# Moving the w3 weight load from the SyncE DMA queue to the ScalarE DMA queue in a one-core decode kernel

## The chip, the cores and the metric

The kernel runs on one core of one Trainium2 chip. The metric is the device time of one execution in microseconds (us), as the median of several executions; a profile of one execution, with every instruction and every DMA packet, goes with each kernel. When two kernels are compared by a ratio, it is the mean time of the one kernel's runs over that of the other's in the same rounds, so it is not quite the ratio of the medians that are quoted beside it.

## The reference, cut to what matters

One token (sequence length 1) goes through two branches that are added: attention over a key/value cache of 65,536 positions in 4 groups, and an MLP.

```python
x  = A_x                                    # 1 x 1 x 1024
xn = _layernorm(x)
return x + _A_ref(xn, k_cache, v_cache, wq, wo) + _B_ref(xn, w1, w2, w3, w4)

# A: q = xn @ wq; softmax(q k / sqrt(128)) v for 32 heads over 4 cache groups; @ wo
# B:
h  = _gelu(_layernorm(x) @ w1)
g0 = jnp.pad(h[:, :, 0*c:1*c], ((0, 0), (1, 0), (0, 0)))[:, :S, :]   # and three more shifts
hs = jnp.concatenate([g0, g1, g2, g3], axis=-1) @ w2
x1 = x + hs
h2 = _gelu(_layernorm(x1) @ w3) @ w4
return x1 + h2
```

All tensors are bfloat16. The bytes: wq 8.4 MB, w3 7.3 MB, w1 and w2 2.1 MB each, 8 key and 8 value blocks of 8.4 MB each, wo 8.4 MB, w4 7.3 MB. That is 169.87 MB for one token, each byte used once.

## The kernel before

Everything that comes from memory passes through three large buffers ("slots", `SLOTS = 3`) in one fixed order. When a matrix or a block has been used up, `done` frees its slot and the next load of the stream is issued into it. All the large loads are issued by the SyncE queue; only the 2 KB row x comes through the ScalarE queue.

```python
    stream = ["wq", "w3", "w12"]
    for u in range(NU):                      # NU = 8 blocks
        ...                                  # cut: the last block has wo between K and V
            stream += [("K", u), ("V", u)]
    stream.append("w4")

    class Stream:
        def pump(self):
            while self.next < len(stream) and self.held < SLOTS:
                ...                          # cut: take the next one
                self.load(it)
        def done(self, it):
            self.tiles.pop(it)
            self.held -= 1
            self.pump()
        def load(self, it):
            t = big.tile([P, ROW], BF16, name="big")
            self.tiles[it] = t
            go = nc.sync.dma_start
            if it == "wq":
                go(out=t[:], in_=A_wq.rearrange("(p c) n -> p (c n)", c=DC))
            elif it == "w3":
                go(out=t[:, 0:DC * F], in_=B_w3.rearrange("(p c) f -> p (c f)", c=DC))
            elif it == "w12":
                go(out=t[:, 0:DC * D], in_=B_w1.rearrange("(p c) n -> p (c n)", c=DC))
                go(out=t[:, DC * D:2 * DC * D], in_=B_w2.rearrange("(m c) n -> m (c n)", c=DC))
            ...                              # cut: wo, w4
            else:
                kind, i = it
                g, b = divmod(i, NB)
                cache = A_k_cache if kind == "K" else A_v_cache
                go(out=t[:], in_=cache[0, g, b * UKEYS:(b + 1) * UKEYS, :].rearrange("(p ct) d -> p (ct d)", p=P))
    ...
    nc.scalar.dma_start(out=x_row[0:1, :], in_=A_x[0, 0:1, :])
    st.pump()
```

So the first key block waits for the slot of wq, the first value block for that of w3, and the second key block for that of w1 and w2. The three projections run in this order:

```python
    def compute_wq():
        psq = ps_S.tile([P, SUBS, 512], F32, name="psq", tag="sc")
        row_matmul(psq, xn_rep, ...)
        st.done("wq")                        # first K block is issued here
        ...                                  # cut: evict, transpose, place the queries
    def compute_w3():
        psh = ps_S.tile([P, SUBS, 512], F32, name="psh", tag="sc")
        row_matmul(psh, xn2_rep, ...)
        st.done("w3")                        # first V block is issued here
        ...
    compute_wq()
    compute_w3()
    compute_w12()                            # second K block is issued at its end
    for u in range(NU - 1):
        compute_k(u)
        compute_v(u)
```

## Time and profile before

| | before |
|---|---|
| median | 400.91 us (400.76 to 401.95, 3 runs) |
| span of the profiled execution | 398.6 us |
| bytes read | 169.87 MB, 426 GB/s over the span |
| busy share of the span | DMA engines 98.9%, PE (TensorE) 57%, DVE (VectorE) 53%, ACT (ScalarE) 7% |

These lines are from the page of the kernel before: the span, the busy share of the 16 DMA engines in 40 slices of the span (in tenths), the DMA queues with packets, megabytes and share of the engines' span (q1 is SyncE's, q10 is ScalarE's), and the chain of work that ended last, by engine.

```profile
span 398.6 us, 2575 instructions
...
DMA  9998999999999999999999999999999998999996
...
q1 hardware_dynamic: 4128, 169.87, 98.9%
...
q10 hardware_dynamic: 6, 0.00, 0.0%
HBM read 169.87 MB, written 0.00 MB: 426 GB/s over the span
...
DMA 56%; DVE 21%; PE 17%; ACT 2%; another core or an unknown queue 2%; issue 1%; SPq 0%; DVEq 0%; ACTq 0%
```

The engines are busy in every slice, down to the last one. PE and DVE each work little more than half of the time. So the kernel looks bound by the load stream; experiment 8 tests this.

The next lines are the first issues of the SyncE queue in order of time (start in us, duration, source line).

```profile
0.00 0.37 SPq L174 DMA_DIRECT2D big<-in_A_wq_dram  x1
0.78 0.33 SPq L176 DMA_DIRECT2D big<-in_B_w_dram  x1
1.16 0.42 SPq L178 DMA_DIRECT2D big<-in_B_w_dram  x1
1.63 0.53 SPq L179 DMA_DIRECT2D big<-in_B_w_dram  x1
27.00 0.33 SPq L193 DMA_DIRECT2D big<-in_A_k_cache_dram  x1
51.36 0.33 SPq L193 DMA_DIRECT2D big<-in_A_v_cache_dram  x1
57.77 0.33 SPq L193 DMA_DIRECT2D big<-in_A_k_cache_dram  x1
```

The four weight loads are in the queue within 2.2 us. The first key block is issued at 27.0, the first value block at 51.4, the second key block at 57.8. In the DMA records 15 of the 16 engines end their last packet of the first key block between 66.9 and 67.6 us and the last one at 68.9, so the first value block was in the queue some 16 us before it was needed.

The projections of wq and w3 and the first work on the first key block (DVE transposes it) in the timeline, with the idle time of the engine before them and what ended it:

```profile
21.99 4.98 PE L290 MATMUL psq<-big,ln_rep_a 128*32 128x512 bf16 x64 [3.73 <-DMA big<-in_A_wq_dram]
...
38.90 12.43 PE L290 MATMUL psh<-big,ln_rep_b 128*32 128x512 bf16 x64 [8.87 <-DMA big<-in_B_w_dram]
...
69.41 8.77 DVE L360 STREAM_TRANSPOSE big<-big 128x4096 f32<-128x4096 f32 x2 [15.70 <-DMA big<-in_A_k_cache_dram]
```

### The profile page before, as it was taken

How to read it: one execution, taken by the hardware profiler on the slowest of the kernel's cores; microseconds unless marked ns; L12 is line 12 of the kernel's file. 1: busy time of each engine (PE TensorE's matmuls, PEld its weight loads, DVE VectorE, ACT ScalarE, POOL GpSimd, SP SyncE). 2: the span in 40 equal slices, each digit the busy share in tenths (PEclk: the TensorE clock that was granted, in tenths of full speed). 3: DMA queues.
4: the chain of work that ended last, by engine and by line, in shares of the span. 5: the costliest groups of instructions: out<-in, count | busy, mean ns of one | idle time of the engine just before them, and what ended most of it. 6: DMA issues, size and time to landing. Idle time of an engine off the chain costs nothing.

```text
span 398.6 us, 2575 instructions
## 1 busy us (share of the span) xinstructions
PE 225.4 (57%) x1360; PEld 44.0 (11%) x866; DVE 210.7 (53%) x160; ACT 27.1 (7%) x35; POOL 5.8 (1%) x29
## 2 busy tenths in 40 slices
PE   0251960591569238733974296519462955394986
PEld 0210000010100010011001010200020101010132
DVE  0610010974296559633963795269439942894141
ACT  1001020003000200020002000200110001002000
POOL 2000000000000000000000000000000000000000
PEclk9995996596869787966695889679956896698799
DMA  9998999999999999999999999999999998999996
GB/s 421 421 443 376 446 427 480 454 421 421 416 428 427 421 467 449 427 421 427 423 441 421 447 454 434 416 427 421 441 436 427 447 447 383 416 462 424 413 432 257
DMA packets 4144, 170.03 MB, mean 427 GB/s; under 512 B 419, under 2 KB 421, under 8 KB 678
## 3 DMA queue, kind: packets, MB, share of 16 engines
q1 hardware_dynamic: 4128, 169.87, 98.9%
q8 instruction: 9, 0.15, 0.2%
q14 instruction: 1, 0.01, 0.0%
q10 hardware_dynamic: 6, 0.00, 0.0%
HBM read 169.87 MB, written 0.00 MB: 426 GB/s over the span
## 4 chain that ended last, share of the span: by engine, by line
DMA 56%; DVE 21%; PE 17%; ACT 2%; another core or an unknown queue 2%; issue 1%; SPq 0%; DVEq 0%; ACTq 0%
DMA big<-in_A_k_cache_dram 42%; DVE big L360 15%; PE sc L365 11%; DMA big<-in_B_w_dram 8%; DMA big<-in_A_wq_dram 6%; PE oacc L415 4%; DVE p_sb L386 2%; DVE mx L370 2%; ACT p_sb L383 2%; PE psq L290 1%; SPq L187 0%; PE pm_mx L372 0%; DVE m L374 0%; PE pm_mx L379 0%
## 5 line engine op out<-in xcount | busy, mean ns | idle before, releaser
L365 PE MATMUL sc<-big,qdiag 128*128 128x512 bf16 x512 | 129.6, 414 | 66.5 <-DVE big L360 61.0
L360 DVE STREAM_TRANSPOSE big<-big 128x4096 f32<-128x4096 f32 x32 | 139.4, 4413 | 50.1 <-DMA big<-in_A_k_cache_dram 50.1
L415 PE MATMUL oacc<-big,p_sb 128*32 128x512 bf16 x512 | 43.2, 504 | 34.5 <-DVE p_sb L386 34.5
L370 DVE TENSOR_REDUCE mx<-sc 128x1 f32<-128x2048 f32 x8 | 18.3, 2292 | 29.9 <-PE sc L365 29.9
L365 PEld LDWEIGHTS <-qdiag 128*128 128x128 bf16 x128 | 13.2, 103 | 178.3 <-issue 145.7
L383 ACT ACTIVATE p_sb<-sc,nball 128x2048 bf16<-128x2048 f32 x8 | 15.7, 1968 | 220.8 <-DVE nball L381 220.8
L386 DVE STREAM_TRANSPOSE p_sb<-p_sb 128x2048 bf16<-128x2048 bf16 x8 | 18.5, 2311 | 18.0 <-ACT p_sb L383 18.0
L415 PEld LDWEIGHTS <-p_sb 128*32 128x32 bf16 x512 | 16.2, 122 | 58.2 <-DVE p_sb L386 35.1
L290 PE MATMUL psh<-big,ln_rep_b 128*32 128x512 bf16 (+1 forms) x64 | 12.4, 942 | 8.9 <-DMA big<-in_B_w_dram 8.9
L455 PE MATMUL o_acc<-big,oT 128*1 128x512 bf16 x48 | 13.2, 447 | 2.4 <-ACT p_sb L383 2.4
L372 PE MATMUL pm_mx<-ident_f,mx 128*1 128x128 f32 x8 | 2.4, 296 | 19.1 <-DVE mx L370 19.1
L424 DVE SCALAR_TENSOR_TENSOR og<-oacc,wb,og 128x512 f32<-128x512 f32 x4 | 3.0, 751 | 18.5 <-PE oacc L415 18.5
L329 DVE STREAM_TRANSPOSE h_row<-h_row 128x896 bf16<-128x896 bf16 x1 | 1.1, 1111 | 22.0 <-ACT h_row L328 22.0
L241 PE MATMUL pm_ln<-ln_rowsum_a,ones_f 128*128 128x1 f32 x2 | 0.6, 348 | 12.8 <-DVE ln_rowsum_a L239 12.8
L437 PE MATMUL pm_e<-ol,sel8big 128*128 128x129 f32 x8 | 2.3, 370 | 9.7 <-DVE ol L436 9.7
L314 POOL COPY qdiag<-qx 32x32 bf16<-32x32 bf16 x16 | 3.3, 204 | 278.7 <-PE sc L365 250.7
L290 PE MATMUL psq<-big,ln_rep_a 128*32 128x512 bf16 x64 | 5.0, 479 | 3.7 <-DMA big<-in_A_wq_dram 3.7
L232 DVE STREAM_TRANSPOSE x_t<-x_row 32x256 bf16<-32x256 bf16 x4 | 2.5, 615 | 8.4 <-DMA x_row<-in_A_x_dram 8.3
L466 DVE TENSOR_TENSOR big<-o_acc,big 1x512 f32<-1x512 f32 x2 | 1.4, 679 | 10.3 <-PE o_acc L455 10.3
L227 PE MATMUL psB<-big,hT 128*32 128x512 bf16 x40 | 4.8, 380 | 1.4 <-DMA big<-in_B_w_dram 1.3
L302 DVE CAST q_row<-psq 128x512 bf16<-128x512 f32 x1 | 0.7, 692 | 7.6 <-PE psq L290 7.6
L379 PE MATMUL pm_mx<-ident_f,rep 1*128 1x1 f32 x8 | 1.8, 229 | 5.0 <-DVE rep L376 5.0
(100 smaller groups left out, 71.9 us busy)
## 6 DMA issues: line engine op xcount, KB each, us to landing
big<-in_A_wo_dram SPq DMA_DIRECT2D x1, 8192.0 KB, 35.7
big<-in_B_w_dram SPq DMA_DIRECT2D x1, 7168.0 KB, 38.1
big<-in_B_w_dram SPq DMA_DIRECT2D x3, 2048.0 KB, 35.5
big<-in_B_w_dram SPq DMA_DIRECT2D x1, 3072.0 KB, 29.5
big<-in_B_w_dram SPq DMA_DIRECT2D x1, 1280.0 KB, 32.2
big<-in_B_w_dram SPq DMA_DIRECT2D x1, 512.0 KB
big<-in_B_w_dram SPq DMA_DIRECT2D x1, 256.0 KB, 33.1
big<-in_A_k_cache_dram SPq DMA_DIRECT2D x8, 42.2
```

What stands on the lines that cost most here:

```text
L227: return nc.tensor.matmul(psB[32 * j:32 * j + 32, :], lhsT=lhsT.to_broadcast([lhsT.shape[0], 32]), rhs=rhs, start=start, stop=False, tile_ ...
L232: nc.vector.transpose(out=x_t[32 * a:32 * a + 32].rearrange("p c j -> p (c j)"), in_=x_row[:, 256 * a:256 * (a + 1)].rearrange("p (i c) -> ...
L290: nc.tensor.matmul(acc[32 * q:32 * q + 32, i, 0:n], lhsT=rep[:, c, :], rhs=cols(c, i, q), start=(c == 0), stop=(c == DC - 1), tile_positio ...
L314: nc.gpsimd.tensor_copy(out=qdiag[at, LEAD:].rearrange("p (x c) -> p x c", x=4)[:, :, 32 * a:32 * a + 8], in_=qx[at, :, 8 * g:8 * g + 8])
L360: nc.vector.transpose(out=words, in_=words)
L365: nc.tensor.matmul(sc[:, e, :], lhsT=qdiag[:, c0:c0 + P], rhs=cols[:, s, e, :, b2, :, r], start=(s == 0 and b2 == 0 and r == 0), stop=(s = ...
L370: nc.vector.reduce_max(out=mx[:], in_=sc[:].rearrange("p e n -> p (e n)"), axis=AX.X)
L383: nc.scalar.activation(out=p_sb[:], in_=sc[:], func=ACTF.Exp, bias=nball[:, b:b + 1], scale=SCALE, accum_out=group["lall"][:, b:b + 1])
L386: nc.vector.transpose(out=flat, in_=flat)
L415: mm = nc.tensor.matmul(oacc[32 * q:32 * (q + 1), :], lhsT=pT[:, e, 32 * t:32 * (t + 1)], rhs=vt[:, :, e, t, :], start=(e == 0 and t < 4), ...
L424: nc.vector.scalar_tensor_tensor(out=og[:], in0=oacc[:], scalar=wb[:, 1:2], in1=og[:], op0=ALU.mult, op1=ALU.add)
L455: nc.tensor.matmul(tail["rows"][0:1, h2, :], lhsT=oT[g][:, j:j + 1], rhs=wt[:, g, j, 512 * h2:512 * (h2 + 1)], start=(g == 0 and j == 0), ...
```

## The change

The intent is to have w3 loaded by the ScalarE queue while the SyncE queue loads wq, w1 and w2. `issue_after` keeps the small load of x ahead of it in the ScalarE queue.

```diff
             elif it == "w3":
-                go(out=t[:, 0:DC * F], in_=B_w3.rearrange("(p c) f -> p (c f)", c=DC))
+                with tc.issue_after(x_load):
+                    nc.scalar.dma_start(out=t[:, 0:DC * F], in_=B_w3.rearrange("(p c) f -> p (c f)", c=DC))
...
-    nc.scalar.dma_start(out=x_row[0:1, :], in_=A_x[0, 0:1, :])
+    x_load = nc.scalar.dma_start(out=x_row[0:1, :], in_=A_x[0, 0:1, :]).ins
     st.pump()
```

The instruction scheduler also reorders a little on PE and DVE around the start: the q matmuls move into the middle of w3's, mask building moves ahead of the second half of the normalization.

## The prediction

> **What bounds it now.** The load stream. The page's DMA line shows 98.9% of the 16 engines' span on one queue (169.87 MB) and 426 GB/s of HBM reads over the span; DMA is 56% of the chain that ended last, while PE is busy 57% and DVE 53%. In the trace's DMA records a 64 KB packet takes 2.418 us and follows its predecessor at once; a 56 KB packet of w3 takes 2.116 us, a 16 KB packet of w1/w2 0.613 us. 169.87 MB over 16 engines at 65,536 B per 2.418 us is 392 us of a 398.6 us span; the rest is the start (1.0 us), slow first packets, scattered losses, and 2.2 us after the last w4 piece (396.4).
>
> **What the change does.** No byte, matmul or eviction is added or removed. One issue (0.33 us) moves from the SyncE to the ScalarE sequencer. The loads share the same 16 engines. The Trainium skill, "DMA: Bandwidth & Descriptors", section "Issuing engines are not separate DMA queues", says issuing from several engines saves only sequencer time; the trace agrees as far as it goes: the 2 KB x row on the ScalarE queue started at 6.84 us behind two 64 KB packets, and its completion write came at 9.34, one further SyncE packet later: packet-by-packet alternation.
>
> So the order changes, not the sum. Estimate from those durations: two wq packets per engine first, then wq and w3 alternate, 4.53 us a pair. wq lands at 6.9 + 6 x 4.53 = about 34 us (before: 21.95), w3 at about 39 (before 38.9), w1/w2 at about 48.5 as before. Projection of wq (5.0 us) then runs 34 to 39 instead of 22 to 27, the first K load is issued near 39 instead of 27.0, w3's matmuls (12.4 us) still run about 39 to 51.5, the first V load is issued near 52 (51.4), the second K near 58 (57.8).
>
> **Critical path.** Nothing of this shows unless the DMA engines run dry. The first K issue at 39 is still 9 us ahead of the end of w1/w2; V at 52 and K at 58 are 10 us or more ahead of the first K's landing (69.3). Scheduler side effects (q transposes inside w3's matmuls, mask building ahead of the normalization) cost 1 to 2 us inside slack: q is needed only at 69. From the first K on, order and tail are unchanged. Possible gain: issue time, already hidden. Possible loss: switching between queues, about 12 switches per engine[...].
>
> **Prediction.** 401.1 us, 80% range 400.0 to 402.4. Faster by over 2%: 0.01; within 2%: 0.97; slower: 0.02.
>
> **What the profile would show.** Two queues with about 162.5 and 7.3 MB, their summed share still about 99%. Median packet durations unchanged (2.42, 2.12 us). wq's issue to landing about 34 us instead of 21.9; w3's about 37 from its issue near 2 us. First K issued 37 to 41 us. DMA share near 1.0 in each stretch to 70 us; first K landing 69 to 70, second near 108. Idle of PE before the wq matmuls grows from 3.7 to about 16 us and before w3's falls from 8.9 to under 3, with no effect on the end.
>
> **What would make it wrong.** Queues not served evenly: SyncE first would land w3 at 49 and delay the first V issue to about 62, still before 69. Interleaved packets running slower than back to back (packets longer than 2.42 us): each 1% over the first 40 us costs 0.4 us. The x row delayed beyond 9.3 us by w3 rows: its chain to the first normalized row takes 10 us and has 14 us of slack now.

## The result

| | before | after |
|---|---|---|
| median, first comparison | 401.43 us (400.76 to 402.64, 4 runs) | 400.69 us (400.57 to 400.90, 4 runs) |
| ratio | | 0.9984, 95% interval 0.9961 to 1.0006: the same |
| span of the profiled execution | 398.6 us | 398.7 us |

The page of the changed kernel, the same lines:

```profile
span 398.7 us, 2579 instructions
...
DMA  9998999999999999999999999999999999999996
...
q1 hardware_dynamic: 3984, 162.53, 94.6%
q10 hardware_dynamic: 150, 7.34, 4.3%
...
HBM read 169.87 MB, written 0.00 MB: 426 GB/s over the span
...
DMA 61%; DVE 19%; PE 18%; ACT 2%; issue 0%; SPq 0%; DVEq 0%; ACTq 0%
```

7.34 MB have moved to q10, the two queues together hold the engines for 94.6 + 4.3 = 98.9% of the span, and the rate over the span is 426 GB/s as before. The larger DMA share of the chain (61% against 56%) is not a change in time: before, the chain runs through the work on the first key block and 7.83 us that the profile gives to "another core or an unknown queue", up to 108.07 us, when the transposes of the second key block begin; after, it runs through the load of the second key block, up to 108.36 us. The first issues, SyncE's first:

```profile
0.00 0.36 SPq L174 DMA_DIRECT2D big<-in_A_wq_dram  x1
0.77 0.33 SPq L179 DMA_DIRECT2D big<-in_B_w_dram  x1
1.15 0.42 SPq L180 DMA_DIRECT2D big<-in_B_w_dram  x1
42.35 0.33 SPq L194 DMA_DIRECT2D big<-in_A_k_cache_dram  x1
57.42 0.33 SPq L194 DMA_DIRECT2D big<-in_A_v_cache_dram  x1
62.97 0.33 SPq L194 DMA_DIRECT2D big<-in_A_k_cache_dram  x1
```

And from the timeline of all engines the issue of w3 by ScalarE, the two projections and the first work on the first key block:

```profile
1.99 0.38 ACTq L177 DMA_DIRECT2D big<-in_B_w_dram  x1
...
36.74 5.57 PE L291 MATMUL psq<-big,ln_rep_a 128*32 128x512 bf16 x64 [18.48 <-DMA big<-in_A_wq_dram]
...
43.72 4.08 PE L291 MATMUL psh<-big,ln_rep_b 128*32 128x512 bf16 x17 [1.41 <-ACT q_row L304]
...
69.22 8.77 DVE L361 STREAM_TRANSPOSE big<-big 128x4096 f32<-128x4096 f32 x2 [9.45 <-DMA big<-in_A_k_cache_dram]
```

The wq projection starts 14.8 us later than before (36.74 against 21.99), and the first three issues after the weights come 15.4, 6.1 and 5.2 us later. The end does not move, and neither does the work on the first key block (69.22 us against 69.41). In the DMA records 15 of the 16 engines end the first key block between 66.9 and 67.5 us and the last one at 68.7, as before. So the next load in the stream, the first value block, still came some 10 us ahead of its need, and the second key block comes behind it in the same queue.

How the two queues share the engines can be read off one engine. These are the DMA records of one of the 16 in the changed kernel (queue, start in us, duration in ns, bytes), from the start until wq has landed. The records do not name the engine; I joined each packet to the one that starts where it ends:

```
q1  1.949  2559 65536      wq
q1  4.507  2420 65536      wq
q10 6.923  2121 57344      w3
q1  9.041  2422 65536      wq
q10 11.460 2116 57344      w3
q1  13.573 2422 65536      wq
...                        (w3, wq, w3, wq, w3, wq, w3 in the same rhythm)
q1  31.707 2420 65536      wq, the last row
q10 34.123 2121 57344      w3
q1  36.241    9     4      wq's completion write
q10 36.247 2116 57344      w3
```

Packets follow one another with no pause, and the queues take turns, one packet each. A pair takes 4.53 us. The Trainium skill, page "DMA: Bandwidth & Descriptors", section "Queues, rings and completion order", says that each engine goes round-robin between the queues that have work, at packet granularity; the trace agrees, with one row of a load (64 KB or 56 KB here) as the packet. It also shows the completion write, 4 bytes and 9 ns long, in a turn of its own: wq's last data ended at 34.13 us, and its completion came 2.12 us later, behind one more packet of w3.

### The profile page after: what moved, and what is told of

Its sections match the earlier page's. It is cut to its first block, busy times and chain, and to the rows that moved or that the text cites. A ratio compares the mean times of both kernels' runs of the same rounds, so it can differ in the third digit from the quotient of the medians.

```text
span 398.7 us, 2579 instructions
## 1 busy us (share of the span) xinstructions
PE 225.7 (57%) x1360; PEld 45.0 (11%) x869; DVE 210.9 (53%) x160; ACT 27.0 (7%) x35; POOL 5.8 (1%) x29
## 3 DMA queue, kind: packets, MB, share of 16 engines
q1 hardware_dynamic: 3984, 162.53, 94.6%
q10 hardware_dynamic: 150, 7.34, 4.3%
## 4 chain that ended last, share of the span: by engine, by line
DMA 61%; DVE 19%; PE 18%; ACT 2%; issue 0%; SPq 0%; DVEq 0%; ACTq 0%
DMA big<-in_A_k_cache_dram 43%; DVE big L361 14%; DMA big<-in_A_wq_dram 9%; DMA big<-in_B_w_dram 8%; PE sc L366 7%; PE oacc L416 4%; PE psh L291 3%; DVE p_sb L387 2%; DVE mx L371 2%; ACT p_sb L384 2%; PE psq L291 1%; PE ps L338 1%; SPq L188 0%; PE pm_mx L373 0%; PE psB L228 0%
## 5 line engine op out<-in xcount | busy, mean ns | idle before, releaser
L416 PEld LDWEIGHTS <-p_sb 128*32 128x32 bf16 x512 | 16.5, 125 | 58.5 <-DVE p_sb L387 35.1
L291 PE MATMUL psh<-big,ln_rep_b 128*32 128x384 bf16 (+1 forms) x64 | 13.4, 939 | 1.4 <-ACT q_row L304 1.4
L456 PE MATMUL o_acc<-big,oT 128*1 128x512 bf16 x48 | 12.6, 430 | 2.4 <-ACT p_sb L384 2.4
## 6 DMA issues: line engine op xcount, KB each, us to landing
big<-in_B_w_dram ACTq DMA_DIRECT2D x1, 7168.0 KB, 38.5
```

Of the source, the lines that this page charges most:

```text
L291: nc.tensor.matmul(acc[32 * q:32 * q + 32, i, 0:n], lhsT=rep[:, c, :], rhs=cols(c, i, q), start=(c == 0), stop=(c == DC - 1), tile_positio ...
L416: mm = nc.tensor.matmul(oacc[32 * q:32 * (q + 1), :], lhsT=pT[:, e, 32 * t:32 * (t + 1)], rhs=vt[:, :, e, t, :], start=(e == 0 and t < 4), ...
L456: nc.tensor.matmul(tail["rows"][0:1, h2, :], lhsT=oT[g][:, j:j + 1], rhs=wt[:, g, j, 512 * h2:512 * (h2 + 1)], start=(g == 0 and j == 0), ...
```

## The experiments

Theory: the time is the bytes over the rate of the 16 engines, plus a fixed start and tail. Issue times are free as long as the engines have packets queued. The change therefore costs and gains nothing, but it spends issue slack: the first value block is issued 6.1 us later. Rivals: the head's compute is on the path and two effects cancel (a faster stream of two queues against a later projection); or the ratio of 0.9984 is a small real gain of two queues; or nothing that happens at the head can ever matter.

For "engines dry" below I added up, from the DMA records between 60 and 100 us, the time in which an engine had no packet of the program, over all 16, and divided by 16. It is 0.00 us in both kernels.

### 1 to 4. The w3 matmuls two and three times over

If slack was spent, the same extra work must hurt the changed kernel earlier and more. The w3 matmuls were repeated in both kernels; a repeat starts its accumulation afresh, so the result stays right (and was). The edit, for both:

```diff
-        row_matmul(psh, xn2_rep, lambda c, i, a: ...)
+        for _ in range(2):                   # and range(3)
+            row_matmul(psh, xn2_rep, lambda c, i, a: ...)
```

Doubled, kernel before:

> The w3 matmuls (12.4 us) are run twice, in the kernel before. Theory (the load stream bounds the kernel; a later issue costs nothing until the 16 engines run dry): the first V load is issued at about 64 us instead of 51.4, still ahead of the end of the first K load at about 68, so no loss: 400.9 us, within 0.3%. Rival (compute at the head is on the critical path): +12 us. No bubble in the packets near 68 us.

Doubled, changed kernel:

> The same doubling in the changed kernel. Theory (the change cost nothing because it only spent issue slack): the first V load moves from 57.4 to about 70.4 us, after the engines have drained the first K load (about 68), so they stand dry for about 3 us and the time is about 404 us (+3 to +4 us), unlike the same doubling in the kernel before (+0). Rival (the change moved no slack): same as the doubled kernel before. Rival (head compute counts): +12 us.

Tripled, kernel before:

> w3 matmuls three times, kernel before. Theory: first V issued at about 76.5 us, engines dry from about 68 to 77.5: about 410 us (+9 to +10 us). Rival (head compute counts): +25 us. Rival (nothing at the head matters): +0.

Tripled, changed kernel:

> w3 matmuls three times, changed kernel. Theory: first V issued at about 83.5 us, engines dry from about 68 to 84.5: about 417 us (+16 to +17 us), that is about 6 to 7 us over the tripled kernel before, which is the slack that the change spent. Rival (no slack spent): equal to the tripled kernel before.

Measured, all against 401.53 us of the kernel before in the same rounds:

| w3 matmuls | kernel | first V issued | engines dry | median | ratio (95% interval) |
|---|---|---|---|---|---|
| twice | before | 63.56 us | 0.07 us | 402.30 us | 1.0019 (1.0004 to 1.0034) |
| twice | changed | 69.98 us | 3.84 us | 405.42 us | 1.0096 (1.0079 to 1.0113) |
| three times | before | 75.83 us | 9.77 us | 412.11 us | 1.0259 (1.0238 to 1.0279) |
| three times | changed | 81.45 us | 15.35 us | 416.86 us | 1.0384 (1.0365 to 1.0403) |

The lines below are the stretch from 68 to 76 us, first of the doubled kernel before, then of the doubled changed kernel, then of the tripled kernel before. Columns: the stretch and its length, busy us (and instructions) of PE, PE weight loads, DVE, ACT and POOL, granted TensorE clock, DMA share, GB/s.

```profile
68.00:76.00 8.00, 5.48 (x30) 0.63 (x6) 6.81 (x2) 1.01 (x1) 0.00 (x0) 0.88 0.93 401
```

```profile
68.00:76.00 8.00, 6.63 (x43) 1.00 (x10) 4.97 (x3) 1.99 (x3) 0.00 (x0) 1.00 0.70 262
```

```profile
68.00:76.00 8.00, 8.00 (x48) 0.74 (x18) 0.00 (x0) 0.16 (x1) 0.00 (x0) 1.00 0.00 0
```

The second column from the right is the one to read: 0.93, 0.70 and 0.00. A first value block issued at 63.6 us finds the engines busy, one issued at 70.0 us finds them idle for some 4 us, and one issued at 75.8 us leaves the whole stretch empty. The first copy of the extra 12 us of work cost the kernel before 0.8 us, the changed one 3.9 us (both against the kernel before; the changed kernel itself was not in these rounds); the second copy cost 9.8 and 11.4 us. So the head's compute is not on the path until the queue runs empty, and then every microsecond counts. The rivals "head compute counts" (+12, +25 us) and "nothing at the head matters" (+0) both fail, and "no slack spent" fails too: with the work tripled, the changed kernel is 4.75 us behind the kernel before, for 5.6 us between their issue times. I had expected 6 to 7 us there.

The 0.8 us of the doubled kernel before were not expected. Its engines were not dry at 68 us. In its trace a packet of the instruction queue (q8, 16 KB, 1.07 us) falls at 395.2 us among the last pieces of w4: the median end of the last piece is 395.17 us (395.16 in the kernel before), but the latest is 397.27 us instead of 396.01. One engine delayed by that packet would fit the 1.2 us; it was seen in one trace and not varied by itself, so it stays an argument.

### 5 and 6. Short rows for w3

If the queues take turns by packets and not by bytes, the size of a row decides the share. w3 was loaded in two pieces of half the columns, so that each row in memory is 3,584 bytes long instead of 57,344. Bytes, queue and order of issue are the same.

```diff
-                    nc.scalar.dma_start(out=t[:, 0:DC * F], in_=B_w3.rearrange("(p c) f -> p (c f)", c=DC))
+                    for f0 in (0, F // 2):
+                        nc.scalar.dma_start(
+                            out=t[:, 0:DC * F].rearrange("p (c f) -> p c f", c=DC)[:, :, f0:f0 + F // 2],
+                            in_=B_w3.rearrange("(p c) f -> p c f", c=DC)[:, :, f0:f0 + F // 2])
```

> w3 on the ScalarE queue in two loads of 3,584 B rows instead of one of 57,344 B rows: same bytes, same queue, same order. Theory (the engines alternate packet by packet between the queues, whatever the packets' sizes, one row is one packet): w3 gets one 3.6 KB packet per 64 KB packet of SyncE, so wq lands near 23 us, w1/w2 near 36, the first K load (issued near 28) near 56, and w3 only when SyncE has nothing left, near 68; its matmuls then run to about 81, the first V load is issued near 81 and the engines stand dry for about 13 us: about 415 us. Rival (queues share by bytes): wq lands near 36 us, w3 near 39, time 401 to 402 us. Rival (16 rows go as one packet): as by bytes.

The control has the same two pieces on the SyncE queue, in the kernel before:

> Control: the same two loads of short rows on the SyncE queue, as in the kernel before. All theories: wq lands at 22, w3 at about 40 (short packets cost about 1 us in all), first V issued near 53; 401 to 402.5 us.

Measured: the changed kernel with short rows takes 417.21 us (ratio 1.0398, 1.0383 to 1.0414), the control 402.36 us (1.0030, 1.0013 to 1.0047). Two of SyncE's issues and a later stretch of the changed kernel with short rows:

```profile
29.12 0.33 SPq L197 DMA_DIRECT2D big<-in_A_k_cache_dram  x1
82.30 0.33 SPq L197 DMA_DIRECT2D big<-in_A_v_cache_dram  x1
```

```profile
69.00:83.00 14.00, 13.58 (x73) 2.15 (x39) 0.29 (x1) 0.69 (x2) 0.81 (x4) 0.88 0.01 1
```

Again the records of one engine show the turns: a wq packet of 2,418 ns, one w3 packet of 140 ns, a wq packet, and so on. wq's last completion write is at 22.7 us (21.6 before), the first key block has its data at 55.5 us, and w3's second piece lands only at 68.9 us, when SyncE has nothing else queued. Its matmuls then hold back the first value block until 82.3 us, and the engines stand dry for 15.1 us. The mechanism is shown, and the time is 2.2 us above the expected one. Sharing by bytes fails (it expected 401 to 402 us), and so does the idea that 16 short rows travel as one packet. The control confirms that short rows alone cost about 1.2 us.

So the change as it was made is neutral partly because its rows are nearly as long as wq's.

### 7. Taking away the PSUM wait

In the changed kernel w3's matmuls start at 43.72 us, after wq's matmuls and the two copies (DVE, then ACT) that evict them, though w3 has landed at 40.5 (issued at 1.99, 38.5 us to landing by the page). The wq projection was moved to two other PSUM tiles:

```diff
-        psq = ps_S.tile([P, SUBS, 512], F32, name="psq", tag="sc")
-        row_matmul(psq, xn_rep, ...)
+        psq = [ps_M.tile([P, 512], F32, name="psq", tag="pm") for _ in range(2)]
+        ...                                  # the same 64 matmuls into psq[i]; evictions likewise
```

> Changed kernel, with the wq projection accumulating in two other PSUM tiles, so that w3's matmuls need not wait for its eviction. Theory: w3's matmuls start right after wq's last one instead of 1.4 us later, the first V load is issued near 56 us instead of 57.4, and the time does not move (400.7 us, within 0.3%), because the slack hid it. Rival (the PSUM wait costs time): 1.4 us faster.

Measured: 400.62 us, ratio 0.9984 (0.9969 to 0.9999), the same as the changed kernel's ratio. From its timeline:

```profile
36.69 6.48 PE L303 MATMUL psq<-big,ln_rep_a 128*32 128x512 bf16 x64 [18.66 <-DMA big<-in_A_wq_dram]
43.00 6.32 PE L291 MATMUL psh<-big,ln_rep_b 128*32 128x512 bf16 x29
```

w3's first matmul now follows wq's last one with no gap, and the first value block is issued at 56.53 us instead of 57.42. That is 0.9 us of the expected 1.4, because the wq matmuls took 6.5 us in this run instead of 5.6. The time did not move: slack again.

### 8. Fewer bytes

With one position, the shifted rows are zero, so the w1 and w2 branch adds exactly nothing. Leaving out its two loads and matmuls takes 4.19 MB off the stream and keeps the result right (it was checked against the reference). The first w4 matmul then has to start the accumulation that w2's matmuls started.

```diff
-    stream = ["wq", "w3", "w12"]
+    stream = ["wq", "w3"]
...
-    compute_w12()
...
-                row_acc(j, hT[:, c:c + 1], wt[...])
+                row_acc(j, hT[:, c:c + 1], wt[...], start=(c == 0))
```

> Kernel before without the loads of w1 and w2 and their matmuls (with a sequence of one position the shifted rows are zero, so their product adds nothing; the result stays right). Theory (bytes over the rate of the engines bound the kernel): 4.19 MB less is 16 packets of 0.613 us less on each engine, 9.8 us: 391 us (-2.4%). Rival (compute chain bounds it): -6 us or less, or nothing.

Measured: 390.64 us, ratio 0.9735 (0.9719 to 0.9751), that is 10.6 us less in the medians where 16 packets of 0.613 us per engine are 9.8 us. (The profiles agree with the 9.8: the loads end at 386.26 us instead of 396.01 and the spans are 388.9 and 398.6 us. The median of the kernel before also holds its longer runs, see experiments 11 and 12.)

```profile
q1 hardware_dynamic: 3840, 165.68, 98.9%
...
HBM read 165.68 MB, written 0.00 MB: 426 GB/s over the span
```

The rate over the span is 426 GB/s, as before. Bytes are what this kernel pays for. This is the one version here that beats both kernels; it is an algebraic saving that holds only for a sequence of one position.

### 9 and 10. Both queues for most of the stream

If two queues moved bytes faster, using both for 134 MB instead of 15 must show it. Every key and value load was cut into two halves of the columns (rows of 32 KB). The control issues both on SyncE, the other kernel issues the second half on ScalarE.

```diff
-                go(out=t[:], in_=cache[...].rearrange("(p ct) d -> p (ct d)", p=P))
+                src = cache[...].rearrange("(p ct) d -> p (ct d)", p=P)
+                go(out=t[:, 0:ROW // 2], in_=src[:, 0:ROW // 2])
+                nc.scalar.dma_start(out=t[:, ROW // 2:], in_=src[:, ROW // 2:])   # control: nc.sync
```

The control:

> Control: kernel before with every K and V load cut into two loads of half the columns (rows of 32 KB instead of 64 KB), both on the SyncE queue. All theories: 401 to 402.5 us (packets of 32 KB, about 1.215 us, cost at most 0.5% more than one of 64 KB).

Two queues:

> As the control, with the second half of every K and V load on the ScalarE queue, so that the two queues alternate during 134 of the 170 MB. Theory (both queues feed the same 16 engines, and switching costs nothing that shows): within 0.5% of the control. Rival (the small gain of the change, 0.16%, comes from two queues moving bytes faster during its 15 MB): about 1.4% (6 us) faster than the control. Rival (a switch costs 0.06 us[...]): about 250 switches per engine, 10 us or more slower.

Measured: the control 402.20 us (ratio 1.0032, 1.0012 to 1.0052), two queues 452.91 us (1.1291, 1.1271 to 1.1310). Two of the three expectations for the second, the theory and the faster stream, were wrong. The third, "10 us or more slower", covers the time but not for its reason, as the packets show; its 0.06 us per switch was an assumption, with no measurement behind it. From its page, the busy share of the DMA engines in 40 slices, and the queues:

```profile
DMA  9999999999959994999399949996999399958992
...
q1 hardware_dynamic: 4128, 102.76, 54.2%
q10 hardware_dynamic: 2310, 67.11, 34.5%
```

The packets themselves were as fast as before: a 32 KB packet took 1,213 ns in the median, in the control 1,215 ns. And between 60 and 100 us, while the queues alternate, no engine is dry (0.00 us). So there is neither a faster stream nor a price per switch that shows. Most of the time went to standing engines: from the first packet to the end of the loads the 16 engines lacked 45.1 us of work in the mean, and for 37.1 us of it all 16 had none, in seven stretches of 2.4 to 6.8 us, about one for each pair of blocks (the notches in the first line). In the control the mean is 1.6 us, so standing accounts for 43.5 of the 50.7 us.

What stood behind it can be seen but was not taken apart. The two halves of the first key block moved from 31.5 to 51.0 us (ScalarE, which had an empty queue) and from 57.3 to 77.1 us (SyncE, behind w3, w1 and w2), while the value block's second half already ran from 59.7 to 78.3 us. In the control the two halves were complete at 58.5 and 68.2 us. Loads that were in file now overtake one another, and a block is usable only when its later half is there. Besides, the scheduler placed the next key block's transposes on DVE ahead of the row maximum of the present one. In the trace the matmuls of the first key block end at 105.5 us, and their row maximum starts at 116.64, behind two transposes that themselves waited for the second key block until 107.94. How much of the 50.7 us is due to the loads' order and how much to DVE's order stays open.

The Trainium skill, page "DMA: Bandwidth & Descriptors", section "Issuing engines are not separate DMA queues", says that DMAs of different issuing engines run on the same 16 engines and interleave, and that issuing from several saves only the time to issue. The 1,213 against 1,215 ns agree. That a version with two queues took 12.6% longer than its control, as here, is not in it.

### 11 and 12. Is 0.16% real?

The changed kernel and the kernel before were run again, five rounds each, against the kernel before (median 400.95 us, 11 runs). No edit in either.

> The changed kernel again, to settle whether its 0.16% is real. Theory (the change does nothing to the stream): ratio 0.998 to 1.001, interval about 1. Rival (a real gain of about 0.7 us): ratio 0.998 with an interval below 1.

> The kernel before against itself: the noise of the comparison. Ratio 1.000; if the interval lies off 1 by 0.1% or more, a ratio of 0.998 says nothing.

Measured: changed kernel 400.74 us, ratio 0.9985 (0.9972 to 0.9999); kernel before against itself 400.91 us, ratio 0.9994 (0.9980 to 1.0008). By the letter the first result is what the rival expected, a ratio of 0.998 with an interval below 1; but the noise interval itself reaches down to 0.9980. The single runs explain the figures. Of the 11 runs of the kernel before in these rounds, 7 lie between 400.75 and 400.97 us and 4 between 401.64 and 402.00; of the 5 of the changed kernel, all lie between 400.53 and 400.84. Against the runs of the first kind the changed kernel is about 0.1 us faster (the middle one of the 7 is 400.85, the median of the changed kernel 400.74). The 0.15% are mostly the second kind, about 1 us longer, which the kernel before takes in a third of these runs.

What makes the second kind was not tested. A candidate is visible in the traces: in both profiles of the kernel before, a ninth instruction packet comes at 397.8 or 396.8 us, just after the last w4 piece (396.0), and in neither of the changed kernel is there a ninth. Were it a microsecond or two earlier, it would delay one engine by about 1 us, as in the doubled kernel before. But no profile of a 402 us run was taken, and the kernel with the PSUM tiles moved has such a packet at 396.2 us and 4 runs between 400.54 and 400.78. The record also has the span of every run: of the 4 longer runs above, two have 399.8 us, about 1 us more than the others, and two have 398.6 and 398.9 us, so that their extra time lies outside the span from the first to the last instruction. A late last piece of w4 can explain the former two only. So this is an argument, not a result. The equal packet times in both kernels speak against a faster stream; what sets off the longer runs stays open.

## Why the prediction was right

**The bound: right.** 98.9% DMA share before, 94.6 + 4.3% after. Taking out 4.19 MB saved 10.6 us in the medians and 9.75 us of loading in the traces; adding 12 us of matmuls to the kernel before cost 0.8 us.

**Only the order changes: right.** Packets of 64 KB and 56 KB take 2,420 and 2,116 ns in the median in both kernels, and a pair takes 4.53 us as predicted.

**The landing of wq: 34 us predicted, 36.7 measured.** The step that failed is "wq lands at 6.9 + 6 x 4.53". Its last data did end at 34.13 us on the engine shown and at 34.24 on the last one. What was missing is one term: the completion write comes only behind one more packet of w3, 2.12 us later. I had noted this of the x row and not carried it over. (The rest, from the completion write to the matmuls, is some 0.4 us in both kernels.) The first key block was therefore issued at 42.35 us, outside the 37 to 41 that the prediction gave.

**w3's matmuls: 39 to 51.5 predicted, 43.7 to 57.4 measured.** The prediction ran the wq matmuls from 34 to 39 and w3's from 39. It left out that w3's matmuls share the PSUM buffer and wait for the eviction, about 1.4 us, and the late wq moved both; w3's stretch is 1.3 us longer as it now holds the q matmuls and some of w2's. So the first value block was issued at 57.4 us and not at 52, and the second key block at 63.0 and not at 58. Against the predicted 69.3 us for the landing of the first key block, the spare time of the first value block was to be 17 us; against the engines' 67.5 us it was 10, and the end did not move: this error of 5.4 us cost nothing only because it too fell into the slack. PE's idle time before the wq matmuls grew from 3.73 to 18.48 us (16 predicted) and that before w3's fell from 8.87 to 1.41 us (under 3 predicted). The tests with doubled and tripled work show that the slack was real and limited.

**The time: 401.1 us predicted (400.0 to 402.4), 400.69 measured in the first comparison and 400.74 in the second.** The possible loss by switching between queues was not found: the spans are 398.6 and 398.7 us.

**What the prediction did not see.** It named uneven queues as a risk only for SyncE being served first, and put that at no cost ("still before 69"). With short rows exactly such a starving of w3 cost 16 us, because the starved load then lands behind the key block too.

## What to carry to other kernels

As long as one set of DMA engines stays busy from end to end, as in both kernels here, moving a load to a second queue changes only the order in which loads land; look for how far each issue is ahead of the moment at which the engines run dry, since that distance is what the change spends. The queues took turns by packets, and a row that is contiguous on both sides was one packet here, so the row lengths of two queues that compete decide which load comes first. The consumers of this stream take its loads in a fixed order; a second queue gained nothing that could be told from noise here, and in two variants the kernel took 16 and 51 us longer. What did shorten the time was fewer bytes.

## What the Trainium skill lacked or had wrong

- "DMA: Bandwidth & Descriptors", "Queues, rings and completion order": it calls a packet typically 9 to 17 descriptors. Whether a row is one descriptor or several the traces don't show; the unit of a turn was one row of the load, for 64 KB rows (2,418 ns) as for 3,584 B rows (140 ns); with short rows against long ones, one queue got one 3.6 KB packet per 64 KB packet. The page does not say that the row length thus sets a queue's share.
- The same section does not give the delay of a completion write when another queue has work: wq's completion came one w3 packet, 2.12 us, after its last data. The section does say that the semaphore increment lands only after every earlier write of its engine, across queues; that would also put it behind the w3 packet, and no run here tells this from a turn of its own.
- "DMA: Bandwidth & Descriptors", "Rules for kernel authors": spreading DMAs over issuing engines for bandwidth is said not to help. A version with two queues can also be slower: 452.91 us against 402.20 us with equal packet times. There the loads of the two queues overtake one another; how much of the loss is due to that stays open (experiment 10).
- "DMA: Bandwidth & Descriptors", "Issuing engines are not separate DMA queues": issue time is called usually small relative to the DMA. In the control with short rows on SyncE, the two issues of w3 took 15.80 us and the next one 10.83 us, behind wq in the same queue; on the ScalarE queue, with nothing large ahead of them, the same two took 0.61 and 0.80 us, and full-row loads took 0.33 us.
- "Runtime: NRT & Kernel Launch", "Instruction fetch mechanics", has instructions refilled in 16 KiB blocks, at a cost that it calls mostly hidden. It does not say what a block costs the loads: here each 16 KB packet of the instruction queue took about 1 us on one DMA engine, with eight or nine of them in a run. In one trace such a packet fell among the last loads, and they ended at 397.27 instead of 396.01 us; that the packet was the reason was not tested.
